# Attention and a gated convolution block on one core: the DMA transposes start at head pair eight in place of ten, the range flag is read earlier, and the instruction order is rewritten

## The chip, the core and the metric

The kernel runs on one core of a Trainium2 chip. Five engines work from their own in-order queues: PE (TensorE, matrix products and transposes), DVE (VectorE), ACT (ScalarE), POOL (GpSimd) and SP (SyncE, which here only issues DMA). The metric is the device time of one execution in microseconds, lower is better. PEld is PE's loading of stationary operands, which runs beside the products.

## The reference

Batch 8, 12 heads, sequence 448, head size 64. Per head:

```python
q_n, k_n = rmsnorm(q, g_q), rmsnorm(k, g_k)
scores = q_n @ k_n.T / sqrt(64)
attn = softmax(scores)              # row maximum subtracted, denominator + 1e-9
x = attn @ v                        # heads side by side: [8, 448, 768]
```

Then, per batch, with w_in [768, 1024], three taps conv_w [3, 1024] and w_out [1024, 768]:

```python
h = relu(x @ w_in)
c = conv_w[0]*h[t-1] + conv_w[1]*h[t] + conv_w[2]*h[t+1]
out = (h * sigmoid(c)) @ w_out
```

All inputs and the output are float32.

## The kernel before

**Tiling.** Two heads of a batch make a pair; there are 48 pairs, six to a batch. A pair has 896 query rows, seven blocks of 128 that are called slots 0 to 6. The steps of a pair n are:

- `load_k`, `load_q`, `v_load`, then the norms: `square` and `square_sum`, `rsqrt` (a few small operations on a tile `st`), `apply_rms` (into a tile `sq`).
- `qk_transpose` and `qk_hi` turn K, and in some pairs q, on PE through a PSUM bank and copy it to `kT` and `qT` (line 681 is the transpose, line 271 or 273 the copy of K, line 267 that of q).
- `scores` (line 862), then `soft_exp` on ACT (line 887) into a tile `e`, one instruction for each slot, with a constant shift in place of the row maximum and the row sums as its accumulator.
- P = `e` is turned so that `pv` (line 1031) can multiply it with v; then `x_scale`, `x_hi`, `x_lo` divide by the row sums and split x in two float16 halves.

After its six pairs a batch has the block that follows attention: `in_part` (line 1120, 18 products for each of eight parts of the hidden size), relu, convolution, tanh and gate on DVE and ACT, `in_hi` and `in_lo`, and `out_part` (line 1189), `out_evac`, `out_store`.

**Two kinds of pair.** A pair below `WHOLE` (here 0 to 9) is kept in float32: `scores` is one float32 pass, P is turned slot by slot on PE (`p_transpose`, line 939, four instructions a slot) and copied out of PSUM by ACT or DVE (`p_evac`, rows `PT<-bank` of line 267), q is turned on PE, and `pv` is one float32 pass. From pair 10 on a pair is in float16 halves: `p_hi` casts `e` to float16 (line 267, rows `ph<-e` and `PT<-e`), `p_lo` subtracts (line 279, two instructions a slot), and one DMA transpose for each slot turns both halves (`p_turn`, line 931, issued by SP); q is split by `q_hi` and `q_lo` and turned by one DMA transpose (`q_turn`, line 723); K gets a second operation `qk_lo` (line 731); v is split by `v_hi`, `v_lo`, `v_twin`; `scores` and `pv` take three passes. Such pairs load K, q and v two pairs at a time, and spread the reciprocals of their row sums with `sum_spread` on DVE (line 996). `ND`, `WHOLE`, `QTURN` and `SPREAD` set where this begins.

**What sets the order.** The string `ORDER` has one entry for each step of the whole program: which step comes next, on which engine it runs, and which PSUM banks it takes. The program is unrolled in that order, and each engine's queue is its share of it. Each engine waits by semaphores for what it reads, and in a few places DVE and POOL wait for each other by the list `SHARED`.

**The end.** `sum_check`, `range_turn` and `range_top` make one number of all row sums; it is larger than 1 where a general program with true row maxima has to follow. All engines read that number into a register and branch on it.

Of the kernel before, what the change touches and what calls it, by code (L numbers as in the profile page):

```python
# [9 lines left out]
I32 = mybir.dt.int32  # L10
AF = mybir.ActivationFunctionType
ALU = mybir.AluOpType
AX = mybir.AxisListType
# [55 lines left out]
    "HI!*HJ!!HK!!.A$!-l$!.%$!,_#!,a$!-F&!HV!!-c&!/Z#!HL!!HM!!.&#!-f%!-g&!-p$!HN!!.B#!,c#!Ha$!/[$!,b#!"
    "HW$!-^!4-i#!-j#!-m$!-q$!HO$!-r#!-n%!-K!$-L!!-M!!/]#!-k&!/$&!-t$!-x$!Ja#!.J!L.|$!.}#!/^%!.K!E.L!4"  # L70
    "-u$!.M$!-y$!.N$!G/%!Hr!)Hs!!Ht!!Hu!!Hv!!Hd!&He!!-v#!/_#!-o&!.q$!L##!-s&!-w&!G]#!-|#!Hw!!-G#!/a%!"
    "-z#!Hf!!Hg!!Hh!!/b#!/c#!/d#!-{&!.Q$!I#!(G|#!/e#!/f#!.R$!.S#!.O#!/g#!-N#!Hb$!HX$!.U$!Hi!!.($!.Y$!"
# [140 lines left out]
    "Uu#!Uv&!Fk!$Fl#!V1$!V2&!"  # L213
)
ND = [0] * 10 + [7] * 38
WHOLE = 10
QTURN = 10
SPREAD = 10

# [1209 lines left out]
```

## Time and profile before

| | |
|---|---|
| time, median of 3 runs | 781.51 us (778.93 to 783.52) |
| the profiled execution | 784.36 us, of which the span of its instructions is 782.6 us |
| PE busy | 749.9 us (96% of the span) |
| DVE busy | 657.2 us (84%) |
| ACT busy | 625.7 us (80%) |
| POOL busy | 345.2 us (44%) |
| last instruction shown on an engine | ends at 776.6 us |

The span runs from the first to the last instruction, with the branch at the end and what the engines do to close the program. Busy is the time in which an engine has at least one instruction under way.

### The profile page before, as it was taken

To read this page: it belongs to the slowest core of one execution; us is meant where nothing else is said; L and a number is where in the kernel's file an instruction comes from. 1 tells how busy PE (TensorE), PEld (TensorE's weight loads), DVE (VectorE), ACT (ScalarE), POOL (GpSimd) and SP (SyncE) were. 2 spreads that over 40 slices of the span, in tenths; PEclk is the share of its full clock that TensorE was granted. 3 is DMA by queue.
4 is the path that set the end of the run, shared out by engine and by line. 5 is a ranking of instruction groups with operands and counts; after the bars stand their busy time and mean duration, and the time that the engine had idled before them with its cause. 6 is when DMAs were issued, how large, how long until landed. Compare 5 with 4: busy or idle time off the path is not lost.

```text
span 782.6 us, 16529 instructions
## 1 busy us (share of the span) xinstructions
PE 749.9 (96%) x5279; PEld 400.0 (51%) x5279; DVE 657.2 (84%) x1592; ACT 625.7 (80%) x1482; POOL 345.2 (44%) x538
## 2 busy tenths in 40 slices
PE   3899999999999989999999999999999999999996
PEld 1455555455545545555545554455445554555553
DVE  6998999999889989898899878997899878974731
ACT  3999899989899868898899778987998778970511
POOL 0154436654366126552465524663465435731200
PEclk9999999999999999999999999999999999999999
DMA  9986664598999999999999999999999988783002
GB/s 239 268 207 185 164 133 96 110 183 185 184 191 185 204 182 180 168 176 206 188 188 187 195 193 184 199 186 180 189 167 180 194 188 155 143 148 83 11 1 85
DMA packets 353428, 130.93 MB, mean 167 GB/s; under 512 B 295708, under 2 KB 349748, under 8 KB 353332
## 3 DMA queue, kind: packets, MB, share of 16 engines
q1 hardware_dynamic: 342928, 120.64, 81.0%
q10 hardware_dynamic: 10404, 9.15, 4.6%
q8 instruction: 43, 0.70, 0.4%
q14 instruction: 53, 0.43, 0.2%
HBM read 48.20 MB, written 11.80 MB: 77 GB/s over the span
## 4 chain that ended last, share of the span: by engine, by line
PE 64%; ACT 13%; DMA 9%; DVE 6%; issue 4%; SPq 1%; POOL 1%; ACTq 0%; DVEq 0%; POOLq 0%
PE bank L1189 23%; PE bank L1120 18%; PE bank L1031 10%; PE bank L862 9%; DMA PT<-PT 3%; DMA PT<-ph 3%; PE bank L939 3%; PE bank L681 2%; ACT PT L267 1%; DMA qkf<-in_q_dram 1%; ACT sq L600 1%; ACT ph L267 1%; DVE ph L279 1%; ACT wi L457 1%; DMA gqk<-in_g_k_dram 1%
## 5 line engine op out<-in xcount | busy, mean ns | idle before, releaser
L1120 PE MATMUL bank<-x,wi 128*128 128x448 f16 x1152 | 229.6, 354 | 2.1 <-DVE kT L731 0.7
L1189 PE MATMUL bank<-wo,gring 128*128 128x384 f16 (+1 forms) x1056 | 196.2, 327 | 0.0
L1120 PEld LDWEIGHTS <-wi 128*128 128x128 f16 x1152 | 111.1, 98 | 109.8 <-issue 14.9
L1189 PEld LDWEIGHTS <-gring 128*128 128x128 f16 (+1 forms) x1056 | 101.4, 99 | 68.3 <-issue 14.2
L862 PE MATMUL bank<-kT,qT 64*128 64x448 f16 (+3 forms) x1072 | 126.4, 388 | 6.1 <-ACT e_(19_2_3546 L887 1.9
L1031 PE MATMUL bank<-PT,vp 128*64 128x448 f16 x836 | 86.7, 354 | 1.0 <-DMA PT<-ph 0.5
L279 POOL TENSOR_TENSOR sq<-qkf,st 112x512 f32<-112x512 f32 (+1 forms) x44 | 46.1, 1060 | 53.5 <-DVE st L637 13.5
L1031 PEld LDWEIGHTS <-vp 128*64 128x64 f16 x836 | 46.2, 110 | 38.9 <-issue 11.7
L862 PEld LDWEIGHTS <-qT 64*128 64x128 f16 (+1 forms) x912 | 33.7, 97 | 56.9 <-issue 34.4
L600 ACT ACTIVATE sq<-qkf 128x1024 f32<-128x1024 f32 (+2 forms) x49 | 49.5, 1022 | 6.6 <-DMA qkf<-in_k_dram 4.5
L681 PE MATMUL bank<-ident,sq 128*128 128x128 f32 (+1 forms) x232 | 35.3, 277 | 13.8 <-DVE st L637 11.1
L609 DVE TENSOR_REDUCE st<-sq 128x16 f32<-128x1024 f32 x38 | 45.3, 1211 | 2.6 <-ACT sq L600 2.6
L1189 PE MATMUL bank<-wo,wi 128*128 128x384 f16 (+1 forms) x192 | 46.9, 326 | 0.0
L279 POOL TENSOR_TENSOR qkf<-sq,qkf 112x512 f16<-112x512 f32 x26 | 30.1, 1162 | 24.6 <-ACT c_(1_0_2529 L271 6.3
L681 PEld LDWEIGHTS bank<-ident,sq 128*128 128x128 f32 (+1 forms) x232 | 26.8, 143 | 24.4 <-issue 16.0
L1189 PE MATMUL bank<-wo,carry 128*64 128x384 f16 x192 | 35.5, 329 | 0.0
L279 DVE TENSOR_TENSOR sq<-qkf,st 112x512 f32<-112x512 f32 (+1 forms) x52 | 34.7, 695 | 0.3
L1031 PE MATMUL bank<-PT,v 112*64 112x448 f32 x160 | 32.3, 545 | 0.0
L774 DVE TENSOR_REDUCE vacc<-v 128x1 f32<-128x512 f32 (+1 forms) x48 | 31.6, 675 | 0.3
L1189 PE MATMUL bank<-wo 128*128 128x384 f16 (+1 forms) x96 | 31.3, 326 | 0.0
L1042 DVE TENSOR_TENSOR x<-bank,rB 128x448 f32<-128x448 f32 x38 | 23.6, 622 | 9.1 <-PE bank L1031 7.7
L279 POOL TENSOR_TENSOR x<-x,x 128x448 f16<-128x448 f32 x22 | 22.8, 1037 | 17.4 <-DVE x L267 4.8
(1911 smaller groups left out, 1714.2 us busy)
## 6 DMA issues: line engine op xcount, KB each, us to landing
qkf<-in_q_dram SPq DMA_DIRECT2D x18, 448.0 KB
wo<-in_moe_w_in_dram SPq DMA_DIRECT2D x12, 512.0 KB
gring<-in_moe_w_out_dram SPq DMA_DIRECT2D x16, 384.0 KB
v<-in_v_dram SPq DMA_DIRECT2D x17, 256.0 KB
qkf<-in_k_dram SPq DMA_DIRECT2D x16, 256.0 KB
qkf<-in_k_dram SPq DMA_DIRECT2D x17, 192.0 KB
PT<-ph SPq DMA_TRANSPOSE x178
qkf<-in_k_dram SPq DMA_DIRECT2D x10, 224.0 KB
```

The source lines that it names most:

```text
L267: (nc.scalar.copy if e == "ACT" else elementwise(e).tensor_copy)(dst, src)
L279: elementwise(e).tensor_tensor(dst, a, b, op=op)
L600: nc.scalar.activation(sq, x, AF.Square)
L609: nc.vector.tensor_reduce(st, sq, axis=AX.X, op=ALU.add)
L681: nc.tensor.transpose(ps[:, t * w : (t + 1) * w], x[:, t], ident[:w, :w])
L774: nc.vector.tensor_reduce(keyed(n, old("vacc", b))[:, i : i + 1], keyed(n, old("v", n)).rearrange("p h t d -> p (h t d)"), axis=AX.X, op=A ...
L862: nc.tensor.matmul(ps[u][o, :S], lhs, rhs, start=(i == 0), stop=(whole(m) or i == 2),)
L939: nc.tensor.transpose(ps[:w, kt * P : (kt + 1) * P], e[:, kt * w : (kt + 1) * w], ident)
L1031: nc.tensor.matmul(ps[HALF[h], :S], lhs, pt[:, k, h * S : (h + 1) * S], start=(i == 0 and j == 0), stop=(i == pvs(n)[-1] and j == NB - 1),)
L1042: nc.vector.tensor_tensor(x, ps, r, op=ALU.mult)
L1120: nc.tensor.matmul(ps[:, :S], wi[:, wl, c, fc * P : (fc + 1) * P], old("x", b * NP + c)[:, xl], start=(i == 0), stop=(i == 3 * NP - 1),)
L1189: nc.tensor.matmul(ps[p0 : p0 + m, :NO2], g, wo[:, wl, fc, half * NO2 : (half + 1) * NO2], start=(i == 0), stop=(i == 3 * NFC - 1),)
```

## The change

- `ND`, `WHOLE`, `QTURN` and `SPREAD` follow one number `FIRST = 8`: pairs 8 and 9 become float16 pairs, with loads for both at once.
- The flag is read 30 steps ahead of the end of the order (`LATE`), without the bounds check of the value, in place of after the last step. The branch stays at the end.
- `ORDER` is another string for the whole program.

```diff
-WHOLE = 10
-QTURN = 10
-SPREAD = 10
+FIRST = 8
+ND = [0] * FIRST + [7] * (48 - FIRST)
+WHOLE = FIRST
+QTURN = FIRST
+LATE = 30
+SPREAD = FIRST
...
-        for step, fn in order:
+        for i, (step, fn) in enumerate(order):
+            if i == len(order) - LATE:
+                flag = nc.values_load(
+                    top[0:1, 2:3].bitcast(I32),
+                    skip_runtime_bounds_check_because="a float that is not negative",
+                )
             taken[:] = placed[step]
...
-    flag = nc.values_load(top[0:1, 2:3].bitcast(I32), min_val=0, max_val=0x7FFFFFFF)
     with tc.If(flag > 0x3F800000):
```

Lines from 217 on stand 3 lower in the changed file. Counted in the two programs, without the general one, where the numbers differ most (a float32 product of the program is two rows of the trace):

| engine, operation | before | after |
|---|---|---|
| PE, P transposes (line 939) | 280 | 224 |
| PE, q transposes (line 681, 112 rows wide) and K transposes of float16 pairs (128) | 80 and 152 | 64 and 160 |
| PE, `pv` in float32 and in float16 | 80 and 836 | 64 and 880 |
| SP, DMA transposes of P and of q | 266 and 38 | 280 and 40 |
| DVE, `p_lo` (pairs of instructions) | 147 | 157 |
| POOL, `p_lo` (pairs of instructions) | 119 | 123 |
| ACT, casts of P | 218 | 235 |
| ACT and DVE, `p_evac` | 50 and 20 | 42 and 14 |
| ACT and DVE, copies of K | 31 and 17 | 38 and 10 |

And on ACT alone, up to the last exponential of pair 16:

| ACT, up to the last exponential of pair 16 | before | after |
|---|---|---|
| casts of P | 41 | 58 |
| `p_evac` | 50 | 42 |
| copies of K | 12 | 16 |
| other casts (x, q, two kinds of gate tile) | 26 | 29 |
| `v_hi`, weight split (line 479) | 5 and 7 | 6 and 8 |
| short copies (`in_carry`, `v_twin`) | 8 | 11 |
| relu and first convolution tap | 25 | 23 |
| DMA issues of loads, stores and row sums | 10 | 8 |

PE around pair 8 (tiles `e_(8_..`: P of pair 8; `kT_1173,qT_1177`: its K and q), before:

```order
L939 MATMUL bank<-ident,e_(8_1_1266 112x128 x4
L862 MATMUL bank<-kT_1173,qT_1177 128x448 x2
L1031 MATMUL bank<-PT_71,v 64x448 x8
L378 MATMUL bank<-ident,wred_out 128x128
L939 MATMUL bank<-ident,e_(8_2_1278 112x128 x4
L939 MATMUL bank<-ident,e_(8_3_1295 112x128 x4
L862 MATMUL bank<-kT_1173,qT_1177 64x448 x2
```

The same place after the change (`kT_1175,qT_1140` are pair 8, `sq_877` and `sq_915` the K of pairs 8 and 9):

```order
L942 MATMUL bank<-ident,e_(7_3_1117 112x128 x4
L865 MATMUL bank<-kT_890,qT_929 128x448 x2
L684 MATMUL bank<-ident,sq_877 128x128 x4
L942 MATMUL bank<-ident,e_(7_4_1131 112x128 x4
L684 MATMUL bank<-ident,sq_915 128x128 x4
...
L865 LDWEIGHTS qT_1140
L865 MATMUL bank<-kT_1175,qT_1140 128x448
...
L1034 LDWEIGHTS vp_1209
L1034 MATMUL bank<-PT_70,vp_1209 64x448
```

The transposes of pair 8's P and q are gone from PE; its scores and `pv` are float16 passes with a weight load each.

ACT in pair 8, before:

```order
L887 ACTIVATE e_(8_2_1278,raw<-bank,lift 128x448
L267 COPY PT_71<-bank 112x4x128
L267 COPY PT_70<-bank 112x4x128
L887 ACTIVATE e_(8_3_1295,raw<-bank,lift 128x448
L1128 ACTIVATE bank<-bank 128x448
L457 ACTIVATE wo_84,wamax<-wo_84 128x384
```

and after:

```order
L890 ACTIVATE e_(8_2_1265,raw<-bank,lift 128x448
L270 COPY PT_71<-bank 112x4x128
L270 CAST ph_74<-e_(8_2_1265 128x448
L274 ACTIVATE c_(0_0_1276<-bank,cwb_1159 128x448
...
L890 ACTIVATE e_(8_3_1298,raw<-bank,lift 128x448
L460 ACTIVATE wo_84,wamax<-wo_84 128x384
L1131 ACTIVATE bank<-bank 128x448
```

Casts of pair 8's P stand there between the exponentials, beside copies that still belong to pair 7.

The end of SP's queue, before:

```order
L1203 DMA out_dram<-c_('o'_7_3_1_9969 128x384
L1203 DMA out_dram<-c_('o'_7_1_1_9972 128x384
L1203 DMA out_dram<-c_('o'_7_3_0_9977 128x384
L1395 TENSOR_LOAD top
L1395 ISA x2
L1396 COMPARE_AND_BRANCH
```

and after:

```order
L1206 DMA out_dram<-c_('o'_7_0_1_9935 128x384
L1387 TENSOR_LOAD top
L1206 DMA out_dram<-c_('o'_7_3_1_10008 128x384
L1206 DMA out_dram<-c_('o'_7_1_1_9998 128x384
L1206 DMA out_dram<-c_('o'_7_3_0_10012 128x384
L1206 DMA out_dram<-c_('o'_7_2_0_10025 128x384
L1206 DMA out_dram<-c_('o'_7_2_1_10028 128x384
L1206 DMA out_dram<-c_('o'_7_1_0_10022 128x384
L1403 COMPARE_AND_BRANCH
```

The load of the flag moved ahead of the last six stores, and two instructions between it and the branch are gone. PE's own transpose for the flag, its last instruction before, stands well ahead of the last output products after.

## Rows read from the trace of the kernel before

**Rows 1.** The page: busy time of each engine, share of the span, instructions.

```profile
PE 749.9 (96%) x5279; PEld 400.0 (51%) x5279; DVE 657.2 (84%) x1592; ACT 625.7 (80%) x1482; POOL 345.2 (44%) x538
```

**Rows 2.** Busy time by stretch: stretch, length, then each engine; clock, DMA share, GB/s.

```profile
26.00:167.00 141.00, 138.16 (x873) 76.38 (x871) 132.41 (x311) 135.19 (x330) 71.40 (x96) 1.00 0.65 161
167.00:245.00 78.00, 76.10 (x552) 39.77 (x551) 68.54 (x169) 70.29 (x169) 39.83 (x62) 1.00 1.01 188
245.00:700.00 455.00, 448.79 (x3312) 236.48 (x3311) 401.98 (x975) 388.75 (x922) 220.53 (x352) 1.00 1.02 182
700.00:783.00 83.00, 75.71 (x498) 41.43 (x496) 35.12 (x77) 17.28 (x34) 10.44 (x14) 0.98 0.19 52
```

**Rows 3.** The chain that ended last, 57 to 167 us, by line.

```profile
by line: PE bank L1120 25.2%; PE bank L1031 23.0%; PE bank L862 20.6%; PE bank L939 19.4%; PE bank L681 5.4%; PE bank L1189 4.4%; ACT e_(3_4_634 L887 0.6%; DVE PT L267 0.6%; DVE wo L407 0.5%; PE bank L378 0.3%; issue 0.1%; DVEq L267 0.0%
```

**Rows 4.** The same chain, pieces of float32 pairs: start, length, what.

```profile
64.41 2.62 PE bank L862 x16
...
82.12 0.77 PE bank L681 x8
...
90.82 3.16 PE bank L1031 x16
93.98 1.45 PE bank L939 x12
```

**Rows 5.** The same chain later, float16 pairs and hidden-part products.

```profile
532.53 2.20 PE bank L1031 x22
534.73 2.22 PE bank L862 x24
...
715.57 27.24 PE bank L1120 x144
```

**Rows 6.** ACT's waits by releaser, 26 to 245 us: total, times, longest.

```profile
ACT e_(12_0_2022 L887 <- PE bank L862: 1.9, 1, 1.9
ACT PT L267 <- PE bank L939: 1.9, 5, 1.1
...
ACT e_(13_5_2364 L887 <- PE bank L862: 0.2, 1, 0.2
```

**Rows 7.** ACT's groups by form: mean ns of one after the busy time.

```profile
L267 ACT COPY PT<-bank 112x512 f32<-112x512 f32 x50 | 28.7, 610 | 1.9 <-PE bank L939 1.9
L271 ACT ACTIVATE kT<-bank,G 128x448 f16<-128x448 f32 x24 | 15.2, 634 | 1.3 <-PE bank L681 1.2
```

**Rows 8.** Timeline of ACT at 401 us, two casts in a row: start, length.

```profile
401.21 0.55 ACT L267 CAST gring<-c_(3_2_5037 128x448 f16<-128x448 f32 x1
401.67 0.56 ACT L267 CAST gring<-c_(3_3_5085 128x448 f16<-128x448 f32 x1
```

**Rows 9.** The instructions of line 931, SP's DMA transposes of P: min/median/max ns.

```profile
L931 SPq DMA_TRANSPOSE PT<-ph x178: 1220/1248/3702, 148.4 to 705.3; - x178
```

**Rows 10.** Lines 1395 and 1396, flag and branch: duration ns, first and last start.

```profile
L1395 SPq TENSOR_LOAD <-top x1: 531/531/531, 776.7 to 776.7; - x1
L1395 SPq FUSED_REGOPS  x1: 187/187/187, 777.3 to 777.3; - x1
...
L1396 PEldq COMPARE_BRANCH  x1: 4422/4422/4422, 776.7 to 776.7; - x1
...
L1396 SPq COMPARE_BRANCH  x1: 57/57/57, 777.6 to 777.6; - x1
```

**Rows 11.** Timeline, the last instructions shown: start, length, idle before and releaser.

```profile
775.69 0.58 ACT L271 ACTIVATE c_('o'_7_3_0_9977<-bank,vsc 128x384 f32<-128x384 f32 x1 [4.85 <-PE bank L1189]
...
776.29 0.33 SPq L1203 DMA_DIRECT2D out_dram<-c_('o'_7_3_0_9977  x1
```

**Rows 12.** Timeline of PE at 286 us.

```profile
286.00 0.72 PE L862 MATMUL bank<-kT,qT 64*128 64x448 f16 x5 [1.89 <-ACT e_(19_2_3546 L887]
...
288.03 8.00 PE L1120 MATMUL bank<-x,wi 128*128 128x448 f16 x33
```

**Rows 13.** Busy time by stretch, the columns of rows 2.

```profile
280.00:300.00 20.00, 17.52 (x110) 8.45 (x110) 16.19 (x45) 13.21 (x34) 7.40 (x16) 0.91 1.07 187
```

More of the change, by code (lines that the diff above doesn't have):

```diff
@@ new lines @@
+    "!1#!$J%!$N!#$O$!%*#!$K!$$L$!!;#!$~#!%!%!%a$!%+#!!<#!!9&!!>&!!=$!%,#!$R!B$U$!%-#!%##!%.%!$X$!%9#!"
+    "%$#!$S!V&:&!&;&!$V!*$Y!+$[$!$_$!!?#!$]!#$W$!$Z$!$a!$%s#!%/%!%0#!!@#!!D#!!E#!!A#!!C&!%1#!!F#!%5#!"
+    "!H&!%6!%%%#!&D&!&~&!(P&!!I#!%2%!&k&!!G$!$^$!$b$!%7$!$T!L$c$!%3!)%4$!%b#!!J#!$f$!!N#!!O#!&<$!%:!l"
+    "!K#!!M&!!P#!!R&!$i$!!B$!!S#!$l%!&=#!$d!#%>$!%c%!$m#!$n#!$e$!%;!8%A$!$g!&!Q$!!T#!%d#!%e#!!U#!!W&!"
+    "&l&!%f#!%D$!!X#!%g#!!Y#!%h#!$o&!%i%!$h#!%j#!!Z#!%k#!%l%!&E#!(!#!$j!)%?!(%@$!(Q#!%o%!!%%!$k$!!^#!"
@@ new lines @@
+    "&A#!!_#!(R#!!]&!!a#!!c&!%<!l%G$!#(&!$p&!!d#!!e#!#)&!(F&!(G&!%=!.%B!%%J$!%C$!%E!(%H!)%M$!%F$!%I$!"
+    "%m!&%P$!%n$!%S#!%p!*%q$!!h#!![$!%T#!!i#!$q&!%K!+%N!%%Q!#%L$!%t!V%u!9!V$!%O#!%U#!%R$!%v!l&>%!(S!#"
+    "!#%!(T#!%w$!%z$!!b$!!l#!!j#!!f#!!m#!!p#!!q#!!n#!!r#!#*#!#+#!&B!(&m$!%}$!&C$!%x!)&?!%&@$!&#$!#/#!"
+    "#,#!!L$!#.&!#0#!&&$!!k$!$r!#%y$!({&!%{!$%Y!(&*$!!&%!!g$!!s$!&n#!#-$!(H%!$s#!%V&!(I#!&o#!#1#!%~!%"
+    "!o$!%|$!(|&!&p#!)2&!&!$!&$!&&%$!&F!j&q#!#4#!&r#!&-$!&0#!&s#!#5#!&t#!&J$!&G!o&(!%!(%!&+!&&)$!&u#!"
@@ new lines @@
+    "&,$!&.!#&1#!&H!j&M$!&I!B&K!+&/$!&v#!#6#!&w#!&{%!&x%!!t#!(M%!#3&!#8&!!u!#(J%!&P$!&S$!&V$!&2#!&3&!"
+    "&N!$&Y$!&L#!!v#!&O#!)V&!)W&!!x$!)b&!&Q!*&T!)&R#!&U#!&y!+&z$!&|!#&}$!)3#!!w#!(N!%#9#!#:#!(O$!&]$!"
+    "#>#!(K!$(L$!&W!*&Z!)(#!n($!B#;#!#=&!&a#!(}$!#?#!(&$!!y#!&6!$#7$!#@#!(~#!$t%!%W&!%X&!)X$!)Y#!(*$!"
+    "$u%!&X#!&[$!!z$!)!%!)##!)$%!)%%!)c#!(-$!&^!+((!#&4&!&5&!&b#!#C#!)&#!)(#!#B&!#D#!(+!)&_$!()$!(0$!"
+    "*C&!!/%!))#!)*#!(,$!(%!g(U!n(3$!(.!&(1!)(4!*#E#!)+#!#G&!&c#!%Z#!#<$!(6$!)Z%!)^#!!$%!&g!((/$!&d&!"
@@ new lines @@
+    "(2$!*D&!(9$!%[$!(7!%(5$!(Y$!(:!&!*%!(V!c#H#!#I#!*+&!*,&!!{#!#J#!#L&!%]#!!|$!*-$!#M#!(8$!&e&!(]$!"
+    "(a$!&f&!(Z!*&7#!)/%!(;#!(<%!)0!#)1$!*E#!([#!(=#!(^!$(_$!),%!)-!%(W!M).$!(X!l)4!.(d$!*~#!(>#!*.$!"
+    "(g$!&8%!#N#!)[!%!}#!#R#!)]$!(?&!#O#!(j$!#Q&!#S#!&9%!*/#!(@&!#T#!#V&!&h#!!)%!&i%!)_!&*0$!*1#!(A&!"
+    "(b!)(m$!(e!%)a$!!~$!)7$!(B!*(c$!(h!((f$!(i$!(k!+(l$!(p%!&j#!*2#!#W#!(q#!*3#!#X#!*4#!#!#!##$!+l&!"
+    "+m&!#Y#!(n!&#[&!)5!2)6!C)8!+):$!(o$!)=$!);!$(v!&)>!#*5#!#]#!*6#!(r#!(s&!*7%!(C#!(D$!*8%!*9#!#^#!"
@@ new lines @@
+    ")@$!#$#!)9$!#%$!#_#!*:#!*v%!)C$!#P$!#b&!)F$!)<#!)?$!)d!j#Z$!!+%!)I$!+n#!#c#!(t&!(u&!*;#!#A$!+R&!"
+    "#d#!+S&!#&#!!4&!)A!$)h$!(z#!)D!+)B#!)E$!(E%!)G!%#e#!)e!Q)k$!!3&!)f!<)J!)#h#!#K$!#U$!)n$!!2&!*z#!"
+    "#i#!*?%!#g&!)H#!)i!+*{$!)l!%)K#!)R!(#f$!#j#!,I#!#l&!)q$!(w#!(x$!+T&!)j#!)m$!,J#!#a$!)t$!*@%!)L%!"
+    ")M#!!5#!*A%!*B&!,K!),L#!*|%!)o!#(y%!)r!&)p$!)s$!G,#!)g!o)w$!#m#!H~#!#r#!*<!%*=$!#n#!#s#!#o#!#t#!"
+    "*>#!)u!)+U$!+V#!)z$!*w!*+W$!+X#!!,%!#p$!G-!#G.!!-;&!-<&!*m%!G/!!)}%!*F!O*I$!)v$!)N#!+Y#!*n#!*M$!"
@@ new lines @@
+    "G0!!G<!%G1!!!-%!*J$!#2$!G2!!#F$!+Z#!+[%!+]%!#q&!-=#!)~#!*G!9G3$!)x!)*Q$!*K#!+^#!*N#!)y$!+_#!*R$!"
+    "#v#!+a#!G4$!#w#!+b#!#x#!G=!!G>!!){!++c#!+h%!,A%!G?!!)|$!*U$!*O%!*S%!+i%!G@!!#y$!)O&!*!#!GA!!GB$!"
+    "#u$!*x#!GC$!*H!;G5#!*}&!*y#!+!!q*Y$!,E%!)P&!)Q&!)S#!G6#!G7$!GD#!#k$!*&!**^$!+j%!G8#!*V$!GE#!*Z$!"
+    "#z#!#{!(-v#!G9$!#|#!*#&!*c$!#~$!*W#!*[#!Gk!$+d#!!.%!*g#!Gl!!Gm!!*L&!)T$!*P&!GZ!#G:#!G[!!$!#!*$&!"
+    "*T&!*_$!*d$!Gz!)G{!!*e#!GF$!+&$!*%&!.d&!)U#!#}#!*h#!GG#!*a%!+($!+#!X++$!$#$!+,$!,F$!*i#!.e&!.f#!"
@@ L221 @@
+    "V2!!V#$!V$&!VC!!V3!!VR!!VS!!Uy$!V7!!VI!!VJ!!V8!!VK!!V9!!V:!!V;!!V&!!V4$!V(!!V)!!VT$!VU&!V5&!VL$!"
+    "V*!!V+!!V,$!VM&!V<#!V=&!VD#!VE&!V-&!"
+)
+FIRST = 8
[4 more added lines that the diff above has]
+SPREAD = FIRST
 class Ring:
```

356 lines of the change are left out of this document (162 added, 194 removed).

## Prediction

> **What bounds the kernel now.** I read the busy times first: PE has work under way in 749.9 of 782.6 us, DVE in 84%, ACT in 80% of the span [rows 1]. An average over the span hides the stages, so next come the stretches [rows 2]. From 700 us on only PE works: 75.7 of 83 us, ACT 17. From 245 to 700 us PE is busy in 448.8 of 455 us, and ACT and DVE have 66 and 53 us to spare: PE is the bound there. From 26 to 167 us it is tighter: of 141 us PE is busy in 138.2, ACT in 135.2 and DVE in 132.4. All three are within 9 us of full, and pairs 8 and 9, which the change touches, lie in this stretch. From 167 to 245 us ACT still has only 7.7 us free of 78, DVE 9.5.
>
> Which of the three decides is seen in the chain that ended last [rows 3]: between 57 and 167 us over 97% of it is PE. So work taken off PE there shortens the chain, until the chain passes to an engine that is nearly as full. That second point decides this change.
>
> **What leaves PE.** A float32 pair costs PE, by pieces of the chain [rows 4]: scores 2.62, `pv` 3.16, 28 P transposes at 1.45 for twelve 3.38, four q transposes at 0.77 for eight 0.39; together 9.55 us. A float16 pair costs 2.22 + 2.20 = 4.42 us [rows 5]; K's four transposes stay in both. That is 5.1 us a pair, 10.3 us for two. All of it leaves the stretch in which PE is the chain. The rest of PE's products are the same in number.
>
> **What comes to ACT.** Up to the last exponential of pair 16, which stands at the end of the stretch at 245 us, the table of counts gives ACT 20 more casts, 8 fewer copies of turned P, 4 more copies of K, one more `v_hi` and one more weight split, 3 more short copies, two fewer relus or taps, two fewer DMA issues. A cast lasts 0.56 us, but the next starts 0.46 us after it [rows 8], so I take 0.46, and 0.1 us off the other durations [rows 7]: 9.2 for the casts, -4.1 for the copies of P (0.51 each), +2.1 for K (0.53), about +1.3 for `v_hi` and the split and +0.6 for short copies (estimated at two operations of K's size and three half as short or less), -1.0 for relu and tap, -0.7 for two issues (0.33 each, as SP's [rows 11]). Sum +7.4 us, say +7. DVE gains `p_lo`, `qk_lo`, `v_lo` and `sum_spread` of two pairs and loses copies of P and K; by the same counting it is +6 us or a little less up to that point, with 18.1 us free from 26 to 245 us against 13.5 on ACT [rows 2]. So ACT is the tighter one.
>
> **What the stretch to 245 us does then.** Bounds first. If ACT closed every gap it would be done 13.5 - 7 = 6.5 us earlier; if it closed none, 7 us later. PE alone would be 10.3 us earlier, which is beyond what ACT allows if the order keeps them in step. Which gaps close? Ten rows of ACT's waits in this stretch name PE as the releaser, from 1.9 down to 0.2 us, together 8.5 us [rows 6]. These I take as closed, since PE is ahead now. The other 5.0 us are waits on DVE and DMA and time between instructions; I take half as closed, between none and all, because DVE gets busier too and DMA has more to do. So ACT closes 11 of 13.5 us and carries 7 more: the stretch ends 4.0 us earlier, with bounds of -6.5 and +7. After it both orders have the same products left on PE, and PE is busy in 98.6% of what follows up to 700 us [rows 2], so a shift at 245 us reaches the end as it is.
>
> **The DMA side costs nothing by itself.** 16 more transposes hold SP's queue for 1.25 us each [rows 9], 20 us more, but from 26 to 167 us the DMA engines are busy to 0.65, against 1.01 to 1.02 in the stretches behind [rows 2], where the pace and the number of transposes for each pair stay as they are. The cover is that the first P transpose starts only at 148.4 us before, so that the queue has room for two more pairs ahead of it. If the cover failed, `pv` of pair 8 would wait, by at most the 20 us, less what PE finds to do in the first batch's hidden part. I take 0. Loads for two pairs move the same bytes in fewer issues: 0.
>
> **The end.** Before, the chain behind the last evacuation (ends 776.27) is: the store's issue on SP to 776.62 [rows 11], the flag's load 0.53 us, 0.19 us for the bounds check, the branch at 777.6 [rows 10], then 5 us of closing to 782.6. On PE the transpose for the flag, DVE's reduction and the load stand between the last product and a branch of 4.4 us at 776.7. With the flag in a register SP goes from the store to the branch: 0.97 us from 776.62 to 777.6; PE, too, branches about 1 us sooner after its last product. Now PE's load of the flag (about 0.5 us) stands among the last output products; at worst half of the gain is lost. I take -1.0, bounds -0.5 and -1.2.
>
> **Sum.** -4.0 - 1.0 = -5.0 us. On the profiled execution: span 782.6 to 777.6, time 784.36 to about 779.4. That execution stands 2.9 us above the median of the runs, so I set the forecast against the median: 781.5 - 5.0 = 776.5 us. With the bounds of its own choices (ACT's other gaps all or not at all, 2.5 us each way, the end, and 1 to 2 us of stalls that any new order has elsewhere) the likeliest case lies between 773 and 780.
>
> **A clock that can take some of it back.** Where PE waited 1.89 us for an exponential within a stretch of short waits near 286 us, the granted clock fell: 0.91 as a mean from 280 to 300 us, and the 33 products that followed took 8.0 us [rows 12, 13]. At the pace of a later piece of the same kind, 144 in 27.24 us [rows 5], they would take 6.2, so such a stall costs its own length and 1.8 us more. The Trainium skill says the same of the two levels, 1.2 and 2.4 GHz: idle gaps on TensorE throttle its clock (TensorE: Matmul & The Clock Gate, "HAM oscillation"); by that rule, a stage in which PE newly waits for ACT can lose more than ACT's added work. The trace agrees once, at 286 us. It is a part of the last rival below.
>
> **Rivals.**
> - *PE's saving arrives whole.* If the new order lets PE run ahead of the exponentials, or starts ACT's early work sooner, ACT's bound moves and the full 10.3 + 1.0 us come: 781.5 - 11.3 = 770.2. For it: the chain is PE alone from 57 to 167 us. Against it: ACT was 96% busy there and gets more.
> - *The gain is eaten.* ACT closes only the waits on PE, DVE's added 6 us open as much elsewhere, and the stretch ends as before; the end gives 1.0: 780.5. For it: three engines near full rarely close all gaps together.
> - *Slower: ACT becomes the bound between pairs 8 and 13.* None of its gaps closes, +7 us stand in the chain, PE waits in the shadow of it and its clock falls once (+1.8), the end gives back 1.0: 781.5 + 7.8 = 789.3. It decides from the point where ACT closes less than 7 of its 13.5 us. Against it: 8.5 us of those gaps are waits on PE.
> - *A change that does nothing at its place* I give no chance; 56 transposes leave PE in any case.
>
> **How the numbers follow.** Chances: likeliest 0.50, saving whole 0.17, eaten 0.21, slower 0.12. The range that leaves out 2 in 10 reaches from below the whole saving, 768, into the slower case, 786.5. Half a per cent is 3.9 us, about what a measurement of this kernel can tell from no change, so faster means below 777.6. Of the likeliest case (773 to 780) about two thirds lie below it: 0.33, with the whole saving 0.17: 0.50. Same: the rest 0.17, the eaten gain 0.19, in all 0.36. Slower: 0.12 and a little of the eaten gain: 0.14.
>
> **What would show it right or wrong.** In the changed profile PE's busy time should be near 749.9 - 10.3 = 740 us, ACT's about 6 us more. The exponentials of pair 16 should end about 4 us sooner than now, and the distance from there to the end should stay, less 1 us. From 57 to 167 us the chain should show more ACT and DVE than 3%, and ACT's waits on PE should be fewer. Behind the last store SP should branch at once. The forecast is wrong if PE idles more than about 8 us between 80 and 245 us (then the eaten or the slower case holds), if ACT is less than 97% busy there while PE is full (whole saving), or if new stalls behind 245 us outweigh the shift.

## The result: 1.1% slower, and the profile after

The changed kernel takes 791.7 us (median of 4 runs, 789.2 to 793.3), the kernel before beside it 782.2 (778.9 to 783.5): ratio 1.0108, 95% interval 1.0067 to 1.0149, or 8.4 us more. I had forecast 776.5 with a range up to 786.5.

The page of the changed kernel, busy time of each engine:

```profile
PE 749.5 (95%) x5243; PEld 397.0 (50%) x5243; DVE 653.0 (82%) x1599; ACT 634.9 (80%) x1506; POOL 343.1 (43%) x544
```

PE has 36 rows fewer than in [rows 1] and is busy just as long. Its stretches, in the columns of [rows 2] (the number behind POOL's pair is the granted clock):

```profile
26.00:167.00 141.00, 130.25 (x795) 67.36 (x795) 133.40 (x319) 135.79 (x334) 59.32 (x87) 0.97 0.79 178
167.00:245.00 78.00, 77.01 (x549) 40.67 (x547) 69.49 (x177) 72.30 (x174) 38.40 (x63) 1.00 1.01 188
...
80.00:245.00 165.00, 157.34 (x1037) 79.40 (x1037) 150.79 (x369) 157.25 (x375) 78.43 (x121) 0.98 0.91 173
...
140.00:164.00 24.00, 19.64 (x130) 8.49 (x129) 23.23 (x53) 23.93 (x55) 11.63 (x19) 1.00 0.90 158
...
78.90:82.30 3.40, 3.40 (x13) 1.91 (x13) 1.67 (x4) 2.19 (x7) 1.23 (x2) 0.51 0.67 148
164.30:167.70 3.40, 2.74 (x12) 0.99 (x13) 3.40 (x8) 3.40 (x9) 2.73 (x4) 0.50 1.35 192
...
642.10:645.50 3.40, 3.40 (x17) 1.92 (x14) 1.21 (x3) 3.40 (x8) 2.15 (x3) 0.50 1.10 124
```

From 140 to 164 us ACT has 0.07 us free and PE 4.4. From 80 to 245 us PE is free for 7.7 us, against 1.9 in the same window before:

```profile
80.00:245.00 165.00, 163.10 (x1099) 87.02 (x1098) 151.06 (x353) 152.49 (x362) 87.60 (x127) 1.00 0.79 157
```

And the clock stands at 0.50, its lower level (1.2 of 2.4 GHz), for about 3.4 us at a time: three of these places are shown, at 34.6 and 297.4 us are two more, where the trace of before has one up to its last product (at 287.9 us). Each takes up to 1.7 us. This execution is the slowest of the four, with a mean clock of 0.988; the others had 0.994 to 0.996, so five falls are more than the kernel has as a rule. The chain that ended last, 57 to 167 us, is no longer PE's [rows 3]:

```profile
by line: issue 9.0%; PE bank L1123 6.6%; PE bank L865 5.4%; ACT PT L270 4.9%; PE bank L942 4.0%; PE bank L1034 2.9%; ACT ph L270 2.6%; DVE vacc L777 2.1%; DVE st L612 2.1%; DVE wi L406 1.9%; ACT wi L482 1.9%; DVE wo L410 1.8%; DVE x L1048 1
```

Where the time is lost along the way is read from the last exponentials of pairs 7, 10, 16 and 47. ACT's timeline, before (start, length):

```profile
102.30 0.64 ACT L887 ACTIVATE e_(7_6_1131<-bank,lift 128x448 f32<-128x448 f32 x1
152.84 0.63 ACT L887 ACTIVATE e_(10_6_1759<-bank,lift 128x448 f32<-128x448 f32 x1
243.85 0.66 ACT L887 ACTIVATE e_(16_6_2993<-bank,lift 128x448 f32<-128x448 f32 x1
699.88 0.63 ACT L887 ACTIVATE e_(47_6_9351<-bank,lift 128x448 f32<-128x448 f32 x1
```

and after:

```profile
110.22 0.67 ACT L890 ACTIVATE e_(7_6_1190<-bank,lift 128x448 f32<-128x448 f32 x1
158.40 0.63 ACT L890 ACTIVATE e_(10_6_1784<-bank,lift 128x448 f32<-128x448 f32 x1
248.06 0.66 ACT L890 ACTIVATE e_(16_6_3031<-bank,lift 128x448 f32<-128x448 f32 x1
707.36 0.63 ACT L890 ACTIVATE e_(47_6_9411<-bank,lift 128x448 f32<-128x448 f32 x1
```

It is 7.9 us late at pair 7, 5.6 at pair 10, 4.2 at pair 16 and 7.5 at pair 47. What is late at pair 7 is for the most part not lost, since the new order does other work earlier: ACT has been busy for 6.3 us more by then, counted from 26 us (stretches up to pair 7's and pair 16's last exponential and from there to PE's last product, before):

```profile
26.00:103.00 77.00, 74.16 (x469) 41.34 (x468) 72.16 (x174) 74.04 (x190) 33.77 (x45) 1.00 0.72 196
26.00:244.50 218.50, 213.77 (x1419) 115.70 (x1417) 200.44 (x477) 204.98 (x497) 111.24 (x157) 1.00 0.78 170
244.50:776.00 531.50, 525.00 (x3812) 278.36 (x3810) 437.56 (x1053) 406.27 (x957) 230.97 (x366) 1.00 0.90 163
```

and after:

```profile
26.00:110.90 84.90, 80.53 (x487) 44.73 (x485) 79.15 (x193) 80.31 (x206) 29.65 (x44) 0.96 0.72 188
26.00:248.70 222.70, 210.96 (x1380) 109.62 (x1380) 206.28 (x500) 211.78 (x516) 101.34 (x155) 0.98 0.87 182
248.70:785.50 536.80, 526.35 (x3814) 280.36 (x3810) 427.87 (x1039) 407.76 (x962) 237.09 (x373) 0.99 0.89 162
```

At pair 16 both kernels have nearly as many PE rows left (3812 and 3814), so the 4.2 us there are a loss. Up to that point ACT is busy for 6.8 us more, and of its 13.5 us without work 10.9 are left. Behind it, where no pair has changed, another 5.3 us are lost. ACT still waits for PE; the waits of 0.2 us and more that name PE come to 7.7 us up to 249 us, against 8.5 before. The two longest after:

```profile
ACT PT L270 <- PE bank L684: 2.5, 1, 2.5
ACT e_(14_0_2448 L890 <- PE bank L865: 2.3, 1, 2.3
```

At the end the branch comes some 0.05 us after the last store's issue (0.97 before, [rows 10, 11]):

```profile
786.09 0.33 SPq L1206 DMA_DIRECT2D out_dram<-c_('o'_7_1_0_10022  x1
```

```profile
L1403 PEldq COMPARE_BRANCH  x1: 3518/3518/3518, 782.3 to 782.3; - x1
...
L1403 SPq COMPARE_BRANCH  x1: 58/58/58, 786.5 to 786.5; - x1
```

### The profile page after: what moved, and what is told of

It is laid out like the page before. It is cut to its first block, busy times and chain, and to the rows that moved or that the text cites. A ratio compares the mean times of both kernels' runs of the same rounds, so it can differ in the third digit from the quotient of the medians.

```text
span 791.5 us, 16580 instructions
## 1 busy us (share of the span) xinstructions
PE 749.5 (95%) x5243; PEld 397.0 (50%) x5243; DVE 653.0 (82%) x1599; ACT 634.9 (80%) x1506; POOL 343.1 (43%) x544
## 4 chain that ended last, share of the span: by engine, by line
PE 54%; ACT 13%; DVE 8%; DMA 6%; issue 5%; POOL 1%; SPq 1%; ACTq 1%; POOLq 0%; DVEq 0%
PE bank L1192 22%; PE bank L1123 15%; PE bank L1034 7%; PE bank L865 7%; DMA PT<-ph 2%; ACT ph L270 2%; PE bank L684 1%; DMA PT<-PT 1%; ACT PT L270 1%; DVE ph L282 1%; DVE st L612 1%; ACT sq L603 1%; SPq L934 1%; DMA qT<-qkf 1%; ACT bank L1131 1%
## 5 line engine op out<-in xcount | busy, mean ns | idle before, releaser
L1192 PEld LDWEIGHTS <-gring 128*128 128x128 f16 (+1 forms) x1056 | 101.7, 99 | 72.9 <-issue 18.7
L865 PE MATMUL bank<-kT,qT 64*128 64x448 f16 (+3 forms) x1088 | 130.5, 386 | 8.0 <-ACT e_(10_0_1650 L890 1.1
L1034 PE MATMUL bank<-PT,vp 128*64 128x448 f16 x880 | 91.7, 357 | 3.1 <-ACT e_(42_5_8424 L890 2.0
L1034 PEld LDWEIGHTS <-vp 128*64 128x64 f16 x880 | 48.8, 110 | 43.0 <-issue 15.5
L865 PEld LDWEIGHTS <-qT 64*128 64x128 f16 x960 | 36.8, 97 | 64.2 <-issue 41.2
L603 ACT ACTIVATE sq<-qkf 128x1024 f32<-128x1024 f32 (+2 forms) x49 | 49.6, 1025 | 8.4 <-DMA qkf<-in_k_dram 5.8
L612 DVE TENSOR_REDUCE st<-sq 128x16 f32<-128x1024 f32 x40 | 47.5, 1211 | 7.0 <-ACT sq L603 6.6
L684 PE MATMUL bank<-ident,sq 128*128 128x128 f32 (+1 forms) x224 | 34.1, 281 | 14.7 <-DVE sq L282 10.3
L282 POOL TENSOR_TENSOR qkf<-sq,qkf 112x512 f16<-112x512 f32 x29 | 33.8, 1167 | 18.8 <-DVE qkf L270 5.1
L282 DVE TENSOR_TENSOR sq<-qkf,st 128x512 f32<-128x512 f32 (+1 forms) x50 | 34.0, 699 | 0.3
L270 ACT CAST x<-x 128x448 f16<-128x448 f32 x35 | 20.0, 573 | 15.4 <-DVE x L1045 13.8
L1019 DVE SCALAR_TENSOR_TENSOR vp<-v,vsc,vp 128x512 f16<-128x512 f32 x40 | 29.7, 751 | 1.3 <-ACT vp L274 1.1
```

Of the source, the lines that this page charges most:

```text
L270: (nc.scalar.copy if e == "ACT" else elementwise(e).tensor_copy)(dst, src)
L282: elementwise(e).tensor_tensor(dst, a, b, op=op)
L603: nc.scalar.activation(sq, x, AF.Square)
L612: nc.vector.tensor_reduce(st, sq, axis=AX.X, op=ALU.add)
L684: nc.tensor.transpose(ps[:, t * w : (t + 1) * w], x[:, t], ident[:w, :w])
L865: nc.tensor.matmul(ps[u][o, :S], lhs, rhs, start=(i == 0), stop=(whole(m) or i == 2),)
```

## The experiments

All were timed in five rounds beside the kernel before on the same chip. The ratios are not quotients of the medians: for f1 and g1 the medians alone show a smaller gain, 0.1 and 0.8 us.

| run | us | before | ratio (95%) |
|---|---|---|---|
| e1 conversion, old order | 825.8 | 780.8 | 1.0563 (1.0525 to 1.0601) |
| e2 new order, float32 | 814.9 | 780.8 | 1.0438 (1.0393 to 1.0483) |
| e3 new order, then old | 788.6 | 780.8 | 1.0089 (1.0056 to 1.0122) |
| e4 old order, then new | 788.6 | 780.8 | 1.0090 (1.0058 to 1.0123) |
| e5 changed, less ACT | 790.6 | 782.5 | 1.0102 (1.0059 to 1.0145) |
| e6 before, less ACT | 782.2 | 782.5 | 0.9989 (0.9957 to 1.0020) |
| e7 changed, store moved | 792.0 | 782.5 | 1.0117 (1.0071 to 1.0164) |
| e8 before, flag and store | 786.9 | 782.5 | 1.0058 (1.0030 to 1.0085) |
| e9 changed, less ACT and DVE | 790.2 | 781.6 | 1.0099 (1.0071 to 1.0128) |
| e10 before, less ACT and DVE | 784.1 | 781.6 | 1.0025 (0.9995 to 1.0055) |
| e11 before, flag later, store | 780.5 | 781.6 | 0.9980 (0.9950 to 1.0011) |
| e12 changed, SP issues | 804.7 | 781.6 | 1.0285 (1.0239 to 1.0331) |
| f1 before, PE less | 781.4 | 781.5 | 0.9973 (0.9945 to 1.0002) |
| f2 before, ACT and DVE more | 786.0 | 781.5 | 1.0062 (1.0039 to 1.0084) |
| f3 both | 787.9 | 781.5 | 1.0062 (1.0034 to 1.0090) |
| f4 old order, then new from 320 us | 785.6 | 781.5 | 1.0051 (1.0027 to 1.0076) |
| g1 before, store moved | 781.1 | 781.9 | 0.9966 (0.9935 to 0.9996) |
| g2 changed, three issues moved | 791.0 | 781.9 | 1.0104 (1.0053 to 1.0155) |

### Conversion or order: e1 to e4

**e1.** The steps of pairs 8 and 9 are taken from the new order, by the count of other steps ahead of each, and set into the old one.

```diff
-ND = [0] * 10 + [7] * 38
-WHOLE = 10
+ND = [0] * 8 + [7] * 40
+WHOLE = 8
```

> Pairs 8 and 9 in float16, all other steps in the order of before, flag read at the end as before. Theory A (the float16 work of pairs 8 and 9 fills ACT and DVE up to 245 us, PE then waits and its clock falls): about as slow as the changed kernel, 788 to 793 us, with the same extra half-clock stretches. Theory B (the new order by itself is worse): 776 to 779 us, since PE's 10 us are saved and the order is the good one.

Measured 45 us more, far outside both. (This arrangement doesn't compute the reference's values; only its time is used.) **e2** is the reverse:

```diff
-FIRST = 8
+FIRST = 10
```

> The order of the changed kernel with pairs 8 and 9 kept in float32 as before, early flag. Theory A: 780 to 783 us, that is the time of before less the 0.9 us of the flag. Theory B: 787 to 792 us, the new order costs by itself.

It came to 34 us more. SP's waits from 57 to 205 us show a likely part of it (in total, times, longest); the second fence is e1, 80 to 205 us:

```profile
SPq L975 <- DVE rT L971: 22.6, 3, 18.7
```

```profile
SPq L724 <- PE bank L863: 12.8, 2, 12.5
```

SP stands 18.7 us at one store of row sums and 12.5 us at one transpose of q, each put among steps that it wasn't ordered with. That these waits make up the time isn't shown. So these two don't separate the theories. What they show is that the place of the steps around these pairs is worth several times the 5 us in question.

**e3, e4.** Splices at step 1250 (about 190 us, pair 14), with the pairs' kinds of their first part and the flag at the end.

```diff
-e3: steps 1250 to 4640 of the changed kernel's order
+e3: the same steps in the order of before
-e4: steps 1250 to 4613 of the order of before
+e4: the same steps in the changed kernel's order
```

> The changed kernel's order for its first 1250 steps (to about 190 us), the order of before for the rest, flag at the end. Theory A and any theory of the early part: 789 to 793 us (of the 9.5 us lost, those before 190 us stay, plus 0.9 for the flag). Theory C (a part of the loss comes from the order of the later part, 3.3 us between pairs 16 and 47 and 2 us behind): 785 to 788 us.

> The order of before for its first 1250 steps (pairs 8 and 9 in float32), the changed kernel's order for the rest, flag load at the end. Theory A and any theory of the early part: 781 to 784 us, no difference from before. Theory C: 785 to 788 us.

Both halves cost 7 us. Theory A, by which all comes from pairs 8 and 9, falls with e4; the early part costs as well (e3). The two don't add up (7 + 7 - 0.9 for the flag against 8.4), since at the seam of e4 pair 15 falls back at once and in part recovers. Nor does e3's profiled execution show where its loss lies: it is the fastest of six, and its span, 783.0 us, is that of before. e3 also gives PE's saving, from its page, at a mean clock of 0.996 as before:

```profile
PE 743.1 (95%) x5243; PEld 390.7 (50%) x5243; DVE 661.4 (84%) x1612; ACT 634.5 (81%) x1503; POOL 335.1 (43%) x535
```

6.8 us less than [rows 1]. In the changed kernel's own trace this is about used up by the stretches at half clock.

### Relief for the full engines: e5, e6, e9, e10

**e5, e6** leave 14 passes of ACT out of either kernel:

```diff
+            if name == "out" and k > 1:
+                return
             nc.scalar.activation(
                 dst[:, 0, 0, :n], z, AF.Abs, accum_out=amax[:, k : k + 1]
```

> The changed kernel without 14 of the 16 passes on ACT that look for the largest absolute value in w_out; they stand at 96 to 125 us and take 0.64 us each with their accumulators, 9 us of ACT in all. Theory A (ACT is the bound from 110 to 167 us, 56.4 of 57 us busy, DVE close behind with 55.1): PE's waits there shrink from 6.5 us to 2 or less and the half-clock stretch at 164 us goes, 784 to 788 us against 791.7 of the changed kernel. Rival (it is the places of single waits in the order, not the load, or DVE is just as full): 790 to 792 us.

> The kernel before without the same 14 passes on ACT, 9 us of ACT between 64 and 120 us. Theory A: PE is the bound there (100% busy from 80 to 205 us), so 780 to 782 us, no change. Rival (ACT's share sets the early part before, too): 776 to 779 us.

e6 did what theory A says, e5 didn't: a ratio of 1.0102 in place of 1.0108 is 0.5 us, far inside the intervals. Its stretches show a likely reason:

```profile
96.00:125.00 29.00, 28.35 (x176) 14.30 (x175) 28.39 (x76) 23.85 (x57) 15.44 (x23) 1.00 0.81 142
140.00:164.00 24.00, 18.93 (x129) 8.09 (x127) 23.45 (x53) 23.96 (x55) 12.72 (x19) 0.98 0.93 170
```

Where ACT was relieved, PE and DVE were full; where ACT is full, it still was. **e9, e10** relieve both engines nearer to that place:

```diff
         c = old("c", (b, fc))
+        if b == 0 and not general:
+            return
         nc.scalar.activation(c, c, AF.Tanh)
...
         h, w = held["m", ("i", b, fc)], old("cwb", b)
+        if b == 0 and i == 2 and not general:
+            return
```

> The changed kernel with less work on both engines in the hidden block of batch 0: its eight tanh passes (ACT, 0.57 us each) and its eight third convolution taps (DVE, 0.68 us each) are left out; they stand between 110 and 168 us. Theory A2 (there ACT and DVE are both full, 56.4 and 55.1 of 57 us, so that relief of ACT alone bought nothing): PE's 6.4 us of waits between 110 and 167 us shrink to 2.5 or less and the half-clock stretch at 164 us goes, 785 to 788 us against 791.7. Rival (the waits come from the places of steps in the order, whatever the load): 790 to 792 us.

> The kernel before with the same eight tanh passes and eight taps of batch 0 left out. Theory A2: PE is 100% busy from 80 to 205 us, so 781 to 783 us, no change. Rival: a gain of 3 us or more, as far as ACT and DVE set the pace before, too.

By the ratios 0.7 us are gained in the changed kernel and 2 us lost in the one before, neither told from none. ACT is still full, and the same PE wait stands there, 2.29 us in place of 2.63 (stretch and PE's timeline of e9):

```profile
140.00:164.00 24.00, 19.61 (x135) 8.69 (x135) 22.12 (x50) 23.70 (x55) 13.75 (x20) 1.00 0.90 162
```

```profile
163.18 0.81 PE L1196 MATMUL bank<-wo,gring 128*128 128x384 f16 x4 [2.29 <-ACT e_(11_0_1831 L890]
```

An output product waits there for an exponential of pair 11, whose bank it takes. In the new order a few per cent of load taken off don't undo such a wait; theory A2 is not borne out for that order.

### Single waits of the late part: e7, e8, e11, e12, g1, g2

At 635 us ACT of the changed kernel stands still at a store (timelines of ACT and of PE):

```profile
634.56 0.63 ACTq L565 DMA_DIRECT2D qkf<-in_k_dram  x1
639.20 0.33 ACTq L1206 DMA_DIRECT2D out_dram<-c_('o'_5_1_1_8365  x1
639.62 0.56 ACT L270 CAST ph<-e_(42_4_8391 128x448 f16<-128x448 f32 x1 [4.10 <-DMA rd<-rT]
```

```profile
640.87 1.57 PE L1034 MATMUL bank<-PT,vp 128*64 128x448 f16 x13 [1.99 <-ACT e_(42_5_8424 L890]
```

The store's data was ready; its issue waits for an earlier transfer to land, the casts and exponentials queue behind it, PE idles 1.99 us, and the clock falls at 642.1 us. **e7** issues it earlier:

```diff
 ACT  soft_exp(42, 3)
+ACT  out_store(5, 1, 1)
...
 ACT  v_twin(41)
-ACT  out_store(5, 1, 1)
```

> The changed kernel with one step moved: the store of the output piece 5,1,1 on ACT, which stood 3.7 us waiting at 635.5 us for the store of row sums issued on SP just before, is issued right after its own copy, some 20 steps earlier. Theory D (single waits in the order of the late part cost each their PE wait and a half-clock stretch): the 2.0 us in which PE idles at 638.9 us and the 1.75 us lost at half clock behind it go, 787 to 789 us. Rival (ACT's 3.7 us are only put off, or the transfers share the loss): 790.5 to 792 us.

No change. ACT now stands at the next issue, a load of K, as long, and PE idles 2.87 us (timelines of ACT and of PE, and the stretch behind the wait):

```profile
638.71 0.61 ACTq L565 DMA_DIRECT2D qkf<-in_k_dram  x1
639.36 0.30 ACT L270 COPY vp<-vp 64x128 f16<-64x128 f16 x1 [4.83 <-DMA PT<-ph]
```

```profile
640.92 2.34 PE L1034 MATMUL bank<-PT,vp 128*64 128x448 f16 x22 [2.87 <-ACT e_(42_5_8424 L890]
```

```profile
638.00:700.00 62.00, 59.13 (x428) 30.93 (x426) 52.39 (x120) 55.27 (x134) 34.49 (x52) 1.00 0.89 156
```

The clock doesn't fall this time.

**e8** moves the like store of before (281 us), and makes and reads the flag early, as the change does:

```diff
 ACT  soft_exp(18, 4)
+ACT  out_store(1, 1, 1)
...
 PE   in_part(7, 7, 3, 3)
+PE   range_turn()
...
 DVE  in_conv(7, 2, 1)
+DVE  range_top()
```

> The kernel before with two parts of what the change and the traces suggest: the flag made and read ahead of the end as in the change, and the store of the output piece 1,1,1 on ACT, which stands 3.4 us waiting at 281.5 us for a store of row sums, issued right after its own copy. Theory D: 0.9 us of the end, 1.9 us in which PE idles at 284.1 us and the 1.75 us lost at half clock at 287.9 us go, 775.5 to 778 us against 780 to 782. Rival (stalls move elsewhere): 780 to 781 us, the flag's 0.9 us alone.

Slower by 0.6%. DVE reaches the reading of the flag's bank long before PE reaches its transpose (DVE's timeline):

```profile
736.82 0.29 DVE L382 TENSOR_REDUCE top<-bank 128x1 f32<-128x128 f32 x1 [7.97 <-PE bank L379]
```

**e11** puts that reading some 30 steps behind, after `in_conv(7, 4, 2)`.

```diff
 DVE  in_conv(7, 4, 2)
+DVE  range_top()
```

> The kernel before with the store 1,1,1 issued right after its own copy as in the run before, and the flag made a little later: its transpose on PE after the products of hidden part 7,7 and its reading of the bank on DVE some 30 steps behind, so that DVE doesn't stand 8 us waiting for PE's transpose. Theory D (the store's move gained 4 us up to pair 46, the early flag's place lost 6.5 behind it): 776.5 to 779 us against 781 to 782.5. Rival (the gain by pair 46 was chance, or the end takes it back anyway): 781 us or more.

780.5 against 781.6: a gain of 0.2%, not told from none. **g1** moves the store alone (the first two lines of e8's diff).

> The kernel before with only the store 1,1,1 issued right after its own copy, so that ACT doesn't stand 3.4 us at it at 281 us. Theory D: 1.9 us of PE's idle time and the half-clock stretch behind it go, 777.5 to 779.5 us against 781.5. Rival (other waits and other half-clock stretches take their place, as in most runs here): 780.5 to 782.5 us.

0.3% faster, at the edge of its interval: 2.7 us by the ratio (0.3 to 5.1), 0.8 by the medians, so that the two theories are not told apart. In the profiled execution, the slowest of twelve, PE waits at the same place all the same, now for q's transpose and longer:

```profile
288.69 0.74 PE L862 MATMUL bank<-kT,qT 64*128 64x448 f16 x6 [4.39 <-DMA qT<-qkf]
```

ACT's own wait there is shorter without the store, though: 5.5 us before (first line, 270 to 300 us), 1.5 in g1, e8 and e11 (second line, e11). In e8 and e11 PE waits no longer than 0.6 us there.

```profile
ACT e_(19_2_3546 L887 <- DMA rd<-rT: 5.5, 1, 5.5
```

```profile
ACT e_(19_2_3546 L888 <- DMA rd<-rT: 1.5, 1, 1.5
```

**g2** also moves the two loads of K:

```diff
 ACT  p_hi(42, 2)
+ACT  load_k(46, 0)
+ACT  load_k(46, 1)
 ACT  out_evac(5, 1, 1)
 ACT  soft_exp(42, 3)
+ACT  out_store(5, 1, 1)
```

> The changed kernel with the store 5,1,1 and the two loads of K for pairs 46 and 47, the three issues at which ACT stood 3.7 and 4.2 us, issued some 4 us earlier, ahead of the row sums' store of pair 41. Theory D: ACT's stall at 635 us, PE's 2 to 2.9 us of idle time and the half-clock stretch behind it go, 786 to 789 us against 791.7. Rival (the clump of transfers there is late whoever issues it, and another wait takes the place): 790 to 792.5 us.

No change. ACT passes the loads of K, but stands at the same store again, 4.56 us, though the exponential ahead of it is done at 628 us; PE waits 3.6 us there (timelines of ACT and of PE):

```profile
632.18 0.34 ACTq L1206 DMA_DIRECT2D out_dram<-c_('o'_5_1_1_8367  x1
632.63 0.63 ACT L890 ACTIVATE e_(42_4_8394<-bank,lift 128x448 f32<-128x448 f32 x1 [4.56 <-DMA PT<-ph]
```

```profile
633.41 0.76 PE L865 MATMUL bank<-kT,qT 64*64 64x448 f16 x10 [2.34 <-ACT e_(42_4_8394 L890]
635.40 2.15 PE L1034 MATMUL bank<-PT,vp 128*64 128x448 f16 x10 [1.23 <-ACT e_(42_5_8424 L890]
```

**e12** gives ACT's late issues to SP:

```diff
-ACT  load_k, load_q, v_load, sum_store, sum_load, out_store (52 steps)
+SP   load_k, load_q, v_load, sum_store, sum_load, out_store (52 steps)
```

> The changed kernel with 52 of the 63 transfers that ACT issues (loads, stores, row sums between about 225 and 700 us) issued by SP at the same places of the order. Theory D2 (in the late part ACT stands waiting at its own DMA issues, 3.7 us at 635 us, and whichever issue stands there): the PE wait at 639 us and its half-clock stretch go, 786 to 789 us. Rival (SP, which also issues the DMA transposes, then stands at the same waits and P comes late): 792 us or more.

13 us worse than the changed kernel. In its trace PE waits for no longer than 0.2 us around pair 42 (636 to 670 us), so the stall is gone there, but more is lost elsewhere; that SP, which issues the transposes too, pays for it is the rival's reading and not shown. Theory D, that each such stall can be taken out for its price, is not borne out, but not refuted either: e7 and g2 didn't take ACT's stall away, e12 took it away at a higher price, and g1 took one away and gained an amount that fits both theories.

### The load of pairs 8 and 9 in the old order: f1 to f4

**f1** takes 5.1 us from PE (three of the four blocks of P in a slot are then copies of the first, so its values are not the reference's, nor f3's):

```diff
-        for kt in range(NB):
+        for kt in range(1 if n in (8, 9) and not general else NB):
...
+        if n in (8, 9) and not general:
+            z = keyed(n, held["t", ("p", n, j)])[:, :P].unsqueeze(1)
+            copy(on["p_evac", n, j], turned(n, j)[:, :NB], z.to_broadcast([kp(n), NB, P]))
+            return
```

> The kernel before, in its own order, with only PE's part of the saving: for pairs 8 and 9 one of the four P transposes of a slot is done and copied out four times, so 42 transposes of 0.12 us, 5.1 us of PE, are left out. What the prediction rests on (PE sets the pace from 57 to 167 us): 777 to 778.5 us against 781.6 to 782.5. Rival (ACT and DVE follow so closely that PE's time is handed back to waits): 780.5 to 782.5 us.

**f2** adds the load on ACT and DVE, **f3** does both:

```diff
+        for _ in range(2 if n in (8, 9) and j < 4 and not general else 1):
+            nc.scalar.activation(
+                e, held["s", (n, j)][:, :S], AF.Exp, bias=shift(n, j),
...
     def p_evac(n, j):
+        if n in (8, 9) and j < 5 and not general:
+            v_bound(n)
```

> The kernel before, in its own order, with only the load that the float16 passes add: eight exponentials of pairs 8 and 9 are done twice on ACT (0.84 us each with the accumulator, 6.7 us) and ten of DVE's largest-value passes over v are done again beside the copies of P (0.68 us each, 6.8 us). Load theory (ACT and DVE have no room between 110 and 167 us): 786 to 790 us. Order theory (the order of before has room for it: ACT waits 13.5 us up to 245 us): 781 to 784 us.

> The two edits of the runs before together: the loads that the conversion of pairs 8 and 9 moves, PE 5.1 us less, ACT 6.7 and DVE 6.8 us more, in the order of before and without a DMA transpose more. The prediction's sum: 777 to 779 us. Load theory (the conversion itself is what costs): 785 to 790 us. Order theory (the conversion is about even, the new order with its DMA transposes costs the 9 us): 778 to 783 us.

f1 gains 0.3% by its ratio (2.1 us, between 0 and 4.3), less than half of what left PE and not told from none. f2 and f3 lose the same 0.6% by the ratios, 4.9 us (4.5 and 6.4 by the medians). ACT's timelines, last exponentials of pairs 7 and 10, of f1:

```profile
101.38 0.65 ACT L887 ACTIVATE e_(7_6_1131<-bank,lift 128x448 f32<-128x448 f32 x1
150.96 0.63 ACT L887 ACTIVATE e_(10_6_1717<-bank,lift 128x448 f32<-128x448 f32 x1
```

of f2:

```profile
100.13 0.64 ACT L889 ACTIVATE e_(7_6_1131<-bank,lift 128x448 f32<-128x448 f32 x1
157.03 0.63 ACT L889 ACTIVATE e_(10_6_1777<-bank,lift 128x448 f32<-128x448 f32 x1
```

and of f3, with a stretch of it:

```profile
100.89 0.64 ACT L889 ACTIVATE e_(7_6_1131<-bank,lift 128x448 f32<-128x448 f32 x1
157.77 0.63 ACT L889 ACTIVATE e_(10_6_1735<-bank,lift 128x448 f32<-128x448 f32 x1
```

```profile
110.00:140.00 30.00, 25.11 (x128) 11.55 (x127) 27.28 (x62) 29.50 (x73) 15.19 (x19) 1.00 0.32 74
```

From pair 7 to pair 10 before takes 50.5 us, f1 49.6, f2 56.9 and f3 56.9. Of 6.7 us more on ACT 6.4 arrive at pair 10, and PE's 5.1 us less make no difference to that: in f3 PE is free for 4.9 of 30 us while ACT is busy in 29.5. The doubled exponentials also hold their banks longer, and DVE carries 6.8 us more, so ACT's load, DVE's load and lateness are not told apart here.

**f4** is e4 with the seam at step 2050, about 320 us.

```diff
-steps 2050 to 4613 of the order of before
+the same steps in the changed kernel's order
```

> The order of before up to pair 22 (about 320 us), the changed kernel's order behind it, flag read at the end; pairs 8 and 9 in float32. Order theory (the new order costs in its late part, 7 us between pair 21 and the last product in the profiles): 786 to 789 us. Theory that all of it comes from pairs 8 and 9: 781 to 783 us.

0.5%, 4.0 us, for the new order of the late part alone, where the kernels do the same work. A part of it could be the seam's; but the traces without one agree: from pair 22's last exponential to PE's last product five kernels in the new order (changed, e5, e7, e9, g2) take 446.9 to 449.7 us, eight in the old one (before, e6, e10, e11, f1, f2, f3, g1) 440.7 to 445.9, with 3 to 8 PE rows fewer to do. The wait at 640 us is in f4's trace, too, and the longest there (PE's waits, 320 to 780 us), but this is the slowest of its twelve executions:

```profile
PE bank L1031 <- ACT e_(42_5_8378 L887: 3.5, 1, 3.5
```

## Why the prediction was wrong

**The step that failed** is "ACT closes 11 of 13.5 us and carries 7 more: the stretch ends 4.0 us earlier". ACT did carry 6.8 us more, but it closed 2.6 of the 13.5 us, not 11, and pair 16's last exponential came 4.2 us later. I had counted ACT's waits on PE, 8.5 us, as closed because PE would be ahead; 7.7 us of such waits stand in the changed trace, at other instructions, and PE itself is free for 7.7 us between 80 and 245 us in place of 1.9. So the two engines wait for each other in turn. f3, a stand-in for the conversion in the old order, points the same way: with PE 5.1 us ahead, 6.4 of 6.7 us more on ACT stand in the chain at pair 10, as they do without it. My reading of it, which no run tests by itself: a gap in a queue that runs in order belongs to the instruction behind it, and it is open to other work only where the order has that work at hand.

**The second** is "1 to 2 us of stalls that any new order has elsewhere" and "a shift at 245 us reaches the end as it is". f4 prices the late part of the new order at 4.0 us (interval 2.1 to 5.9), and the changed trace loses 5.3 us behind pair 16. With f3's 4.9 and the flag's 0.9 back that is 8.0 of the 8.4 us measured. This is a sum over kernels of the old order, not a division of the changed one, and the agreement may be chance; e3 and e4 give 7 us for either part and don't add up.

**Sizes.** PE's saving was 6.8 us, not 10.3: I took the pieces of a chain as the price of a pair. By line (before and e3) the transposes of P fell by 7.9 us and `pv` by 1.8, about as priced, but the scores rose by 2.2 where I had them fall by 0.8. The end gave 0.9 of 1.0, as said. DMA transposes were set at 0; no run tells them apart from the order. The fall of the clock was priced rightly (1.8 us, measured up to 1.7), but counted only in a rival and once; in the profiled executions it came four times more than before. The Trainium skill's rule that idle gaps throttle PE (TensorE: Matmul & The Clock Gate, "HAM oscillation") would have weighed against the likeliest case; the page speaks of longer gaps than these. The traces agree in part: the clock fell behind idle times of 1.99 us (638.9 us) and 2.63 us (162.3 us), but not behind 2.87 us in e7.

**The rivals.** "ACT becomes the bound between pairs 8 and 13", 789.3 us, came nearest in place and time, at a chance of 0.12. The mark that I named, PE idle for more than about 8 us between 80 and 245 us, was just missed with 7.7. It still isn't the whole: ACT closed some of its gaps, and more than half of the loss stands behind 245 us. That the time falls near 789.3 us is in part luck, since the rival has nothing behind 245 us.

**Open.** Why relief bought so little in the new order (e5, e9), which speaks against load alone as the cause of the early part, and which places of the order cost the late 4 us. No run has the conversion itself in the old order at fitting places (e1 misplaced it); f3 only stands in for it. No version here beats the kernel before by more than some 0.3%.

## What to carry to other kernels

Where three engines are some 94% busy or more, price a shift of work by the engine that receives it first (of 6.7 us here 6.4 arrived within three pairs, 4.9 at the end); count on little from the engine that is relieved. A hand-tuned order is a part of the result: a new one has a price of its own in stages that the change doesn't touch, and it should be timed without the change. A single stall in such a trace is no bargain by itself; after moving an instruction, look whether the stall has gone at all, and what stands in the same microsecond then, in more than one execution.

## What the runs showed of the hardware

In the changed kernel's trace PE's idle times of 1.99 and 2.63 us had a second price nearly as large: some 3.4 us at half clock behind them, up to 1.7 us lost. It isn't paid each time: e7's trace has an idle time of 2.87 us with the clock at 1.00 behind it. A store issued on ACT kept the engine idle for 4.1 us (changed kernel) and 4.6 us (g2), though its data was ready; near 635 us, where the DMA engines' share is about 1, moving such issues on ACT only changed which transfer was waited for, while near 281 us ACT's wait fell from 5.5 to 1.5 us.
